# The x of three batches leaves attention as one float32 plane and is split where feed-forward first uses it

## The chip, the core and the metric

One core of a Trainium2 chip runs the whole program. The time is the device time of one execution in microseconds, and the kernel before is given by the median of three runs. An execution under the hardware profiler gives the busy times, waits and transfers that are read below.

## What is computed

Attention of 4 batches, 12 heads, 448 positions and 64 channels, in which the heads are mixed with each other before and after the softmax, is followed by a feed-forward layer whose activation is a rational function.

```python
def _attn_ref(q, k, v, w_pre, w_post) -> np.ndarray:
    scale = 1.0 / np.sqrt(q.shape[-1])
    scores = scale * np.matmul(q, k.transpose(0, 1, 3, 2))
    scores = np.einsum('bhij,hg->bgij', scores, w_pre)
    scores = scores - np.max(scores, axis=-1, keepdims=True)
    attn = np.exp(scores)
    attn = attn / (np.sum(attn, axis=-1, keepdims=True) + 1e-09)
    attn = np.einsum('bhij,hg->bgij', attn, w_post)
    return np.matmul(attn, v).astype(np.float32)

def _moe_ref(x, w_in, w_out, a, b) -> np.ndarray:
    h = x @ w_in
    h2 = h * h
    h3 = h2 * h
    P = a[0] + a[1] * h + a[2] * h2 + a[3] * h3
    Q = 1.0 + np.abs(b[0]) * np.abs(h) + np.abs(b[1]) * h2
    g = P / (Q + 1e-06)
    return (g @ w_out).astype(np.float32)
```

x is the output of attention with batches and positions joined: 1792 x 768. w_in is 768 x 2048, w_out 2048 x 768.

## The kernel before

**Order of the work.** The program is a list of operations, each with the engines that may do it, an estimated duration, what it depends on, and a time `at` by which it is due. `Plan.run` goes through them with simulated clocks: whenever an engine is free, it takes of the operations that are ready the one with the smallest `at`. Where several engines are allowed (`ON` names them), the first that is free takes it. What comes out is a fixed order of instructions for each engine; on the chip an engine runs its own order strictly, and an instruction whose operands are late holds up all behind it. `Ring` and `Slot` count the buffers of a pool in the same simulation.

**Attention.** The 1792 rows are cut into 16 tiles T, four to a batch b = T // 4, of 120 rows with one of 88 in each batch (T = 0, 7, 11, 15). For a tile, q times k gives scores in PSUM (L496); ScalarE or VectorE copies them to `st` (L236 and L238), and a DMA shuffles them into `d`, where heads and rows share the partitions. Then the tile goes through in groups of up to two blocks, 92 groups in all: TensorE mixes the heads into `ps_t` or `ps_u` (L565), VectorE takes the row maximum `nm` (L571), ScalarE the exponential `e` with its sum `sm` (L580), GpSimd adds 1e-9 to the sum (L587), VectorE takes the reciprocal `rr` (L591), GpSimd scales the second mixing matrix by it into `krs` (L600), TensorE mixes again with that (L640), and VectorE transposes the result into `aa` (L656). After the last group of a tile `put_av` multiplies by v (L705) into the pair of banks `ps_t` or `ps_u` that the mixing does not use at that time; when it has all three products, ScalarE copies each of two halves (`hv`) into the float32r buffer `xs` (L236, `hi`), VectorE subtracts that from PSUM into the plane beside it (L723, `lo`), and SP stores finished columns to `x_scr` in DRAM (L728).

**Products in pairs.** In feed-forward float32 accuracy comes from pairs: a value is its float32r copy ("hi") plus a remainder ("lo"), and a product is hi x hi + hi x lo + lo x hi. So x stands in two planes per half, `[128, hv, hi/lo, 3, 448]`, and so do the weights `w` and the activation `g`. The weights are prepared along the way from 64-bit inputs: ScalarE and VectorE bring them to `cm` (L405 to L430), ScalarE casts hi (L236), GpSimd subtracts lo (L446). These last make most of GpSimd's work in feed-forward.

**Feed-forward.** There are 64 units: four rounds over the four batches in the orders (0,3,1,2), (2,1,0,3), (3,0,1,2), (2,1,0,3), and four slices of the 2048 channels in each turn. A unit is 18 matmuls of 128x448 into `ps_s` (`m1`, L879), the rational function (ScalarE L892 to L919, VectorE L905 to L929, with `quot` at L929 last), the cast of its result to g's hi on ScalarE or VectorE (L236 or L238), the remainder of g on VectorE (L939), and 18 matmuls with w_out (`m2`, L969), due 2.5 units after the start of the unit's m1, so that the products of later units lie between. Batch 3 stays in `xs` and is the second turn. The others come from `x_scr` through `put_load_x(n)` (L860): n = 1 is batch 0 into the first score buffer, now named "x", due 45 us before the planned end of attention, n = 2 is batch 1 into "x", n = 3 is batch 2 into "xs"; n = 4 to 9 load a batch again in later rounds. A load takes both planes of a batch, 2.75 MB, at once:

```python
nc.sync.dma_start(out=t.bitcast(F32), in_=x_scr[b])
X[n] = t
```

PSUM has eight banks: `ps_s` and `ps_a` two each, `ps_t` and `ps_u` two each, which hold scores in attention and the sums over four units in feed-forward. Weight pieces come back from `w_scr` as `w` (L843), and a one-element memset on GpSimd (L833) holds each of the first of these loads back until an exponential late in attention is done.

Of the kernel before, what the change touches and what calls it, by code (L numbers as in the profile page):

```python
# [28 lines left out]
NT = 4 * B  # L29
# [178 lines left out]
def subs(n, on=("dve", "pool")):  # L208
# [5 lines left out]
    "s": ('act', 'dve'), "d_hi": ('act', 'dve'), "d_lo": ("dve", "pool"), "p": ("act", "dve"), "x_hi": ("act",),  # L214
    "g_hi": ("act", "dve"), "g_lo": ("dve",),
}


def dma(nbytes):
    return nbytes / 300e3  # L220
# [21 lines left out]
def mixed_attention_then_rational_ffn(ctx: ExitStack, tc, q, k, v, w, wmix, mask, a, b2, out):  # L242
# [447 lines left out]
    def put_av(T, pr, at):  # L690
# [19 lines left out]
        def part(hv):  # L710
            return box[hv][:, 0:3 * n].rearrange("p (r w) -> p r w", r=3)[:, :, 0:r]

        def hi(hv):
            def fn(eng):
                if hv == 0 and T % 4 == 0:
                    Xs[b] = sb["xs"].tile([128, 2, 2, 3, S], F32R, tag="xs", name="xs")
                move(nc, eng, Xs[b][:, hv, 0, :, c0:c0 + r], part(hv))
            return fn

        def lo(hv):  # L720
            def fn():
# [15 lines left out]
        for hv in range(2):  # L737
            deps, after = [o], []
            if hv == 0 and T % 4 == 0:
                deps.append(R["xs"].take())  # L740
            else:
                after.append(xs_op[b][0])
            h_ = add(copies(3 * n, False, on=ON["x_hi"]), 0, hi(hv), deps, at=at, after=after)
            l_ = add("dve", dve(3 * n), lo(hv), [h_], at=at)
            xs_op.setdefault(b, []).append(h_)
            x_done.setdefault((b, hv), []).append(l_)
            R["ps_" + holds[T]].uses[slots[hv].k].append(l_)
            if T % 4 > 1:
                last = T % 4 == 3
                cols, done = (slice(c0, S), x_done[b, hv][3:]) if last else (slice(0, c0 + r), x_done[b, hv][:])  # L750
                for hl in range(2):
                    when = at + (3.0 if last else 5.0) + (1.6 if last else 4.0) * (2 * hl + hv)
                    s_ = bulk(0.45, store(hv, hl, cols), done, at=when, nbytes=128 * 3 * max(cols.stop - cols.start, 240) * 4, late=1.0, since=when - 1.0)
                    x_st.setdefault(b, []).append(s_)
                    R["xs"].uses[b].append(s_)

    xs_op, x_done = {}, {}
    x_st = {}

# [91 lines left out]

    def put_load_x(n, at):
        b, name = homes[n]

        def fn():
# [4 lines left out]
            nc.sync.dma_start(out=t.bitcast(F32), in_=x_scr[b])  # L860
            X[n] = t
        x_ld[n] = [add(
            "sp", 0.63, fn, [R[name].take(), R["d"].uses[NT - 2] if n == 1 else op_rest, x_st[b]], at=at, extra=dma(128 * 2 * KD * S * 4))]
        x_use[n] = R[name].uses[-1]

    def put_unit(u):
# [254 lines left out]
```

## Time and profile before

| quantity | before |
|---|---|
| median of three runs | 831.5 us (831.42 to 833.6) |
| the profiled execution: its time | 830.89 us |
| its span | 829.1 us, granted clock 0.996 |
| TensorE (PE) busy | 801.0 us, 97% |
| weight loads (PEld) | 598.0 us, 72% |
| VectorE (DVE) | 690.6 us, 83% |
| ScalarE (ACT) | 502.4 us, 61% |
| GpSimd (POOL) | 222.2 us, 27% |
| DMA | 155.46 MB, mean 187 GB/s |

Attention fills the span up to about 350 us, feed-forward the rest. Busy time counts only instructions that compute, weight loads run beside matmuls, and a share is a mean over stages that have different limits. SP only issues transfers, which the DMA engines carry out.

### The profile page before, as it was taken

The numbers are of one execution on the slowest core, as the hardware profiler recorded it, in microseconds if no ns is written. First come the engines' busy times: TensorE is split into PE (matmuls) and PEld (weight loads), VectorE is DVE, ScalarE is ACT, GpSimd is POOL, SyncE is SP. The second block draws the span as 40 slices with busy tenths as digits, with TensorE's granted clock in tenths as the row PEclk, the third lists the DMA queues.
The fourth block names the chain that finished last, engine by engine and source line by source line (L and its number), as shares of the span: only waits on it lengthen the run. The fifth ranks groups of instructions, "written<-read, shape, count | busy, mean of one in ns | idle before, by whom it ended". The sixth has DMA issues, their size and how long they took to land.

```text
span 829.1 us, 23254 instructions
## 1 busy us (share of the span) xinstructions
PE 801.0 (97%) x9360; PEld 598.0 (72%) x9360; DVE 690.6 (83%) x1252; ACT 502.4 (61%) x1099; POOL 222.2 (27%) x393
## 2 busy tenths in 40 slices
PE   5889999999999999999999999999999999999998
PEld 1244455554554445589999999999999999999997
DVE  5677788887888888888999998999889999677775
ACT  2456666655665566566776775677557677545632
POOL 2224444432444343721111212123212222100000
PEclk9999999999999999999999999999999999999999
DMA  6677878777887675985733255664477634466314
GB/s 201 207 214 224 246 259 265 222 202 231 260 259 212 217 235 171 335 276 210 256 125 101 81 207 133 215 141 104 88 228 192 165 82 67 78 225 231 122 57 156
DMA packets 71900, 155.46 MB, mean 187 GB/s; under 512 B 12560, under 2 KB 52336, under 8 KB 70640
## 3 DMA queue, kind: packets, MB, share of 16 engines
q1 hardware_dynamic: 67736, 141.99, 52.6%
q0 software_dynamic: 3456, 11.01, 8.2%
q8 instruction: 74, 1.21, 0.6%
q10 hardware_dynamic: 600, 0.97, 0.4%
q14 instruction: 34, 0.28, 0.1%
HBM read 77.49 MB, written 37.75 MB: 139 GB/s over the span
## 4 chain that ended last, share of the span: by engine, by line
PE 84%; DMA 6%; DVE 5%; ACT 2%; issue 1%; POOL 0%; SPq 0%; ACTq 0%; DVEq 0%; POOLq 0%
PE ps_s L879 28%; PE ps_u L969 9%; PE ps_t L969 9%; PE ps_a L969 9%; PE ps_s L496 8%; PE ps_a L640 7%; PE ps_t L565 4%; PE ps_u L565 4%; DMA d<-st 4%; PE ps_u L705 2%; PE ps_t L705 2%; DVE nm L571 2%; ACT e L580 2%; DMA kk<-in_k 1%; DVE aa L656 1%
## 5 line engine op out<-in xcount | busy, mean ns | idle before, releaser
L656 DVE STREAM_TRANSPOSE aa<-ps_a 128x448 f32<-128x448 f32 (+1 forms) x184 | 107.8, 618 | 11.6 <-PE ps_a L640 10.8
L879 PE MATMUL ps_s<-d,w 128*128 128x448 f32 x504 | 107.4, 366 | 0.0
L879 PE MATMUL ps_s<-xs,w 128*128 128x448 f32 x504 | 107.1, 366 | 0.0
L236 ACT COPY st<-ps_s 120x448 f32<-120x448 f32 (+1 forms) x120 | 60.4, 533 | 69.2 <-PE ps_s L496 38.3
L496 PE MATMUL ps_s<-kk,q 64*64 64x448 f32 x720 | 94.0, 552 | 8.3 <-DMA kk<-in_k 5.4
L446 POOL TENSOR_TENSOR w<-cm,w 128x384 fp32r<-128x384 f32 x48 | 53.7, 1118 | 177.8 <-ACT w L236 168.4
L600 POOL TENSOR_SCALAR krs<-kpost,rr 128x64 f32<-128x64 f32 x180 | 81.7, 468 | 72.1 <-DVE rr L591 51.3
L879 PEld LDWEIGHTS ps_s<-d,w 128*128 128x128 f32 x504 | 94.3, 188 | 8.7 <-issue 0.9
L879 PEld LDWEIGHTS ps_s<-xs,w 128*128 128x128 f32 x504 | 94.6, 188 | 7.9
L640 PEld LDWEIGHTS ps_a<-e,krs 64*32 64x32 f32 x2880 | 44.7, 106 | 74.4 <-issue 29.0
L640 PE MATMUL ps_a<-e,krs 64*32 64x224 f32 x2880 | 92.6, 355 | 1.6 <-DVE aa L656 0.8
L892 ACT ACTIVATE m<-ps_s,a_sb 128x448 f32<-128x448 f32 x64 | 46.2, 722 | 76.8 <-PE ps_s L879 73.4
L969 PE MATMUL ps_u<-g,w 128*128 128x448 f32 x336 | 84.1, 366 | 0.0
L969 PE MATMUL ps_a<-g,w 128*128 128x448 f32 x336 | 84.1, 366 | 0.0
L969 PE MATMUL ps_t<-g,w 128*128 128x448 f32 x336 | 83.9, 365 | 0.0
L580 ACT ACTIVATE e<-ps_t,nm 128x448 f32<-128x448 f32 x92 | 57.8, 635 | 25.4 <-DVE nm L571 17.1
L580 ACT ACTIVATE e<-ps_u,nm 128x448 f32<-128x448 f32 x88 | 55.3, 635 | 22.0 <-DVE nm L571 18.6
L969 PEld LDWEIGHTS ps_t<-g,w 128*128 128x128 f32 x336 | 63.1, 188 | 5.3
L969 PEld LDWEIGHTS ps_a<-g,w 128*128 128x128 f32 x336 | 63.1, 188 | 5.2
L969 PEld LDWEIGHTS ps_u<-g,w 128*128 128x128 f32 x336 | 63.1, 188 | 5.2
L496 PEld LDWEIGHTS ps_s<-kk,q 64*64 64x64 f32 x720 | 29.5, 135 | 49.4 <-issue 21.5
L915 ACT ACTIVATE ua<-sq 128x448 f32<-128x448 f32 x64 | 37.1, 580 | 33.6 <-DVE sq L912 33.4
(90 smaller groups left out, 1452.7 us busy)
## 6 DMA issues: line engine op xcount, KB each, us to landing
d<-st SPq DMA_DIRECT2D x144, 210.0 KB
cr<-in_w SPq DMA_DIRECT2D x64, 384.0 KB
d<-x_scr SPq DMA_DIRECT2D x5, 2688.0 KB
xs<-x_scr SPq DMA_DIRECT2D x4, 2688.0 KB
o_scr<-o POOLq DMA_DIRECT2D x24, 448.0 KB, 5.7
d<-st SPq DMA_DIRECT2D x42, 157.5 KB
x_scr<-xs SPq DMA_DIRECT2D x12, 540.0 KB
q<-in_q SPq DMA_DIRECT2D x16, 384.0 KB
```

The lines of the kernel that those rows point to most:

```text
L236: eng.copy(o, i)
L446: eng.tensor_sub(t[:, 1, :], box["m"].bitcast(F32), t[:, 0, :].bitcast(F32))
L496: nc.tensor.matmul(box["s"][hh][i0:i1, 0:S], lhsT=Q[T][d, pr, i0:i1], rhs=K[b][d, pr, :], start=True, stop=True)
L565: nc.tensor.matmul(box[r if nt == 2 else 0]["t"][64 * c:64 * c + 64, 0:S], lhsT=kpre[p], rhs=Dt[T][p, kb + c if nt == 2 else kb, :], start ...
L580: nc.scalar.activation(e, box[r]["t"][:, 0:S], AF.Exp, bias=box[0]["nm"][:, r:r + 1], accum_out=box[0]["sm"][:, r:r + 1])
L600: eng.tensor_scalar_mul(box[r]["kr"], kpost, rr)
L640: nc.tensor.matmul(banks[c]["p"][q_:q_ + BT, JH * r:JH * (r + 1)], lhsT=box[r]["kr"][p, m_, :], rhs=box[r]["e"][p, JH * jh:JH * (jh + 1)], ...
L656: nc.vector.transpose(o, src)
L879: nc.tensor.matmul(h[:, 0:S], lhsT=W[fi][:, wi, kk * 128:(kk + 1) * 128], rhs=x[:, kk // 3, xj, kk % 3, :], start=(n == 0), stop=(n == 3 * ...
L892: nc.scalar.activation(new("m"), box["h"], AF.Identity, scale=a_sb[:, 3:4], bias=a_sb[:, 2:3])
L915: nc.scalar.activation(box["ua"], box["vv"], AF.Ln)
L969: nc.tensor.matmul(O[key][:, 0:S], lhsT=W[fi][:, wi, DM + m * 128:DM + (m + 1) * 128], rhs=box["g"][:, gi, :], start=(f == 0 and n == 0), ...
```

## The change

For batches 0, 1 and 2 (`whole`) the output of attention is copied from PSUM by ScalarE as before, but into one plain float32 plane `Y[b]`, one of two halves of the `xs` buffer by b % 2. The VectorE subtractions of these batches fall away (24 of 32). After the last tile of a batch six stores of 128x448 (224 KB each) bring the plane to `y_scr`, 18 in place of 24 stores of pieces to `x_scr`. Batch 3 is unchanged. At the first use of a batch in feed-forward (n = 1, 2, 3) SP loads the plane in two halves into the place of the remainders; ScalarE casts each of the six 128x448 pieces into the place of hi, and GpSimd subtracts that from the plane in place; two stores bring both planes to `x_scr` for the later rounds, which load them as before. The pieces are due 2.0 us apart from 20 us behind the load for n = 1, and 2.6 us apart from 6 us behind it for n = 2 and 3.

Counted over the program: ScalarE gets 18 casts and loses five score copies, which go to VectorE; VectorE also loses two casts of g and gains three copies of o; GpSimd gets 18 subtractions; SP issues six loads of y and six stores of x more, and three loads of x and six stores from attention fewer.

```diff
@@ put_av
+        whole = b < B - 1
+
         def hi(hv):
             def fn(eng):
                 if hv == 0 and T % 4 == 0:
-                    Xs[b] = sb["xs"].tile([128, 2, 2, 3, S], F32R, tag="xs", name="xs")
-                move(nc, eng, Xs[b][:, hv, 0, :, c0:c0 + r], part(hv))
+                    if b == 0 or not whole:
+                        Xs[b] = sb["xs"].tile([128, 2, 2, 3, S], F32R, tag="xs", name="xs")
+                    if whole:
+                        Y[b] = Xs[0].rearrange("p v l k s -> p (v l) k s").bitcast(F32)[:, 2 * (b % 2):2 * (b % 2) + 2]
+                move(nc, eng, Y[b][:, hv, :, c0:c0 + r] if whole else Xs[b][:, hv, 0, :, c0:c0 + r], part(hv))
             return fn
...
+        def store_y(hv, kk):
+            def fn():
+                nc.sync.dma_start(out=y_scr[b][:, hv, kk], in_=Y[b][:, hv, kk])
             return fn
...
-            l_ = add("dve", dve(3 * n), lo(hv), [h_], at=at)
+            l_ = h_ if whole else add("dve", dve(3 * n), lo(hv), [h_], at=at)
...
-            if T % 4 > 1:
+            if whole:
+                if T % 4 == 3:
+                    for kk in range(3):
+                        when = at + 3.0 + 1.6 * (3 * hv + kk)
+                        s_ = bulk(0.45, store_y(hv, kk), x_done[b, hv][:], at=when, nbytes=128 * S * 4, late=1.0, since=when - 1.0)
...
@@ put_load_x
-    def put_load_x(n, at):
+    def put_load_x(n, at, lead=0.0, gap=0.0):
...
+        if b in x_st:
+            x_ld[n] = [add("sp", 0.63, fn, [*free, x_st[b]], at=at, extra=dma(128 * 2 * KD * S * 4))]
+            return
...
+        def hi(hv, kk):
+            def fn(eng):
+                move(nc, eng, X[n][:, hv, 0, kk], X[n][:, hv, 1, kk].bitcast(F32))
...
+        def lo(hv, kk):
+            def fn(eng):
+                x = X[n][:, hv, 1, kk]
+                eng.tensor_sub(x, x.bitcast(F32), X[n][:, hv, 0, kk].bitcast(F32))
...
+        for hv in range(2):
+            got.append(bulk(0.5, load(hv), [*free, y_st[b]], at=at + hv, nbytes=128 * 3 * S * 4, after=got[:1]))
+            parts = []
+            for kk in range(3):
+                when = at + lead + gap * (3 * hv + kk)
+                h_ = add(copies(S, on=ON["x_hi"]), 0, hi(hv, kk), [got[hv]], at=when)
+                parts += [h_, add(subs(S, on=ON["x_lo"]), 0, lo(hv, kk), [h_], at=when)]
+            x_ld[n] += parts
+            s_ = bulk(0.63, store(hv), parts, at=at + lead + gap * (3 * hv + 3) + 2.0, nbytes=128 * 2 * 3 * S * 4)
...
@@ the calls
-        put_load_x(n, at=END1 + UNIT * PH * (held.index(n) - 1) + 1 if n > 1 else END1 - 45.0)
+        if n == 1:
+            put_load_x(n, at=END1 - 45.0, lead=20.0, gap=2.0)
+        else:
+            put_load_x(n, at=END1 + UNIT * PH * (held.index(n) - 1) + 1, lead=6.0, gap=2.6)
```

What this does to the orders is shown at three places; x2 and the like stand for equal instructions in a row, and the line numbers of the changed kernel are shifted by one or more.

VectorE at the end of tile 2, before (L723 is the two subtractions, L571 the row maxima, L238 a score copy):

```order
L591 RECIPROCAL rr<-sm 128x2
L723 TENSOR_TENSOR xs<-ps_u,xs 128x3x120 x2
L571 TENSOR_REDUCE nm<-ps_t 128x2
L656 STREAM_TRANSPOSE aa<-ps_a 128x2x7x32 x2
L571 TENSOR_REDUCE nm<-ps_u 128x2
L238 COPY st<-ps_s 120x448
L591 RECIPROCAL rr<-sm 128x2
L656 STREAM_TRANSPOSE aa<-ps_a 128x2x7x32 x2
```

The same place now:

```order
L592 RECIPROCAL rr<-sm 128x2
L572 TENSOR_REDUCE nm<-ps_t 128x2
L238 COPY st<-ps_s 120x448
L657 STREAM_TRANSPOSE aa<-ps_a 128x2x7x32 x2
L572 TENSOR_REDUCE nm<-ps_u 128x2
L592 RECIPROCAL rr<-sm 128x2
L657 STREAM_TRANSPOSE aa<-ps_a 128x2x7x32 x2
L572 TENSOR_REDUCE nm<-ps_t 128x2
L238 COPY st<-ps_s 120x448
```

The subtractions are gone, the reduction has moved up to their place, and a score copy has moved up behind it.

GpSimd at the end of attention, now (L908 is the subtraction of batch 0, L588 and L601 the norms of the last groups, L854 the memsets that pace the weight loads; before, only the norms and the memsets stand there):

```order
L601 TENSOR_SCALAR krs<-kpost,rr 128x64 x2
L908 TENSOR_TENSOR d<-d 128x448
L588 TENSOR_SCALAR sm<-sm 128x2
L854 MEMSET w_6186 1x1 x2
L908 TENSOR_TENSOR d<-d 128x448
L601 TENSOR_SCALAR krs<-kpost,rr 128x64
L588 TENSOR_SCALAR sm<-sm 128x2
L601 TENSOR_SCALAR krs<-kpost,rr 128x64
L854 MEMSET w_6186 1x1 x2
L908 TENSOR_TENSOR d<-d 128x448
```

Each subtraction now stands ahead of a norm. TensorE at the same place, before, with L879 the first feed-forward product:

```order
L705 MATMUL ps_u<-aa,vv 64x120 x28
L879 MATMUL ps_s<-d,w_6183 128x448 x18
L565 MATMUL ps_t<-d,kpre 64x448 x2
L640 MATMUL ps_a<-e,krs 32x224 x16
L705 MATMUL ps_u<-aa,vv 64x120 x28
L640 MATMUL ps_a<-e,krs 32x224 x16
```

And now:

```order
L706 MATMUL ps_u<-aa,vv 64x120 x28
L566 MATMUL ps_t<-d,kpre 64x448 x2
L641 MATMUL ps_a<-e,krs 32x224 x16
L706 MATMUL ps_u<-aa,vv 64x120 x28
L943 MATMUL ps_s<-d,w_6186 128x448 x18
L641 MATMUL ps_a<-e,krs 32x224 x16
```

The last mixing product, a second mixing and a product with v have moved ahead of the first feed-forward product, which waits for the whole split of batch 0.

ScalarE in feed-forward around units 4 and 5, now (L956 to L983 are the activations of a unit, `CAST d<-d` the casts of batch 1):

```order
L966 ACTIVATE sq<-sq,c_sb,b_sb 128x448
L236 CAST d<-d 128x448 x2
L956 ACTIVATE m<-ps_s,a_sb 128x448
L959 ACTIVATE sq<-ps_s 128x448
L962 ACTIVATE ua<-ps_s,b_sb 128x448
L411 ACTIVATE cm<-cr 128x384
L236 CAST w_6802<-cm 128x384
L979 ACTIVATE ua<-sq 128x448
L966 ACTIVATE sq<-sq,c_sb,b_sb 128x448
L983 ACTIVATE ua<-ua 128x448
L236 CAST d<-d 128x448
```

The casts stand between the activations of running units; before, there is nothing but those and the casts of weights and g.

## Rows read from the trace of the kernel before

**Rows 1.** Windows: from:to length, busy PE, PEld, DVE, ACT, POOL, clock, DMA share, GB/s.

```profile
60.00:310.00 250.00, 241.84 (x5304) 123.92 (x5304) 204.13 (x378) 155.94 (x418) 104.58 (x228) 1.00 0.77 235
375.00:705.00 330.00, 330.00 (x1624) 304.37 (x1623) 310.11 (x566) 225.01 (x426) 70.44 (x68) 1.00 0.53 150
```

**Rows 2.** Waits of TensorE, 60 to 310 us: waiter <- releaser: sum, count, mean.

```profile
PE ps_u L565 <- DVE nm L571: 1.5, 3, 0.7
PE ps_t L565 <- DMA d<-st: 1.4, 1, 1.4
PE ps_t L705 <- issue: 1.3, 1, 1.3
PE ps_u L565 <- DMA kk<-in_k: 1.0, 1, 1.0
PE ps_u L705 <- issue: 0.8, 1, 0.8
...
PE ps_u L565 <- DVE xs L723: 0.5, 1, 0.5
PE ps_t L565 <- DVE xs L723: 0.3, 1, 0.3
```

**Rows 3.** Timeline of VectorE, end of a tile: start, duration, instruction, [wait].

```profile
100.84 0.97 DVE L723 TENSOR_TENSOR xs<-ps_u,xs 128x360 fp32r<-128x360 f32 x2 [0.39 <-ACT xs L236]
101.73 1.08 DVE L571 TENSOR_REDUCE nm<-ps_t 128x2 f32<-128x896 f32 x1
```

**Rows 4.** Timeline of TensorE, right behind.

```profile
103.38 0.98 PE L565 MATMUL ps_u<-d,kpre 64*64 64x448 f32 x8 [0.73 <-DVE nm L571]
```

**Rows 5.** Lines, VectorE, 60 to 310 us: count | busy, mean ns | idle before.

```profile
L238 DVE COPY st<-ps_s 120x448 f32<-120x448 f32 (+1 forms) x45 | 27.5, 617 | 10.8 <-PE ps_s L496 6.8 <-DMA d<-st 3.0 <-PE ps_a L640 0.7
```

**Rows 6.** Lines by shape, ScalarE: the casts of g.

```profile
L236 ACT CAST g<-ua 128x448 fp32r<-128x448 f32 x32 | 18.2, 569 | 26.0 <-DVE ua L929 20.9 <-PE ps_a L969 4.8
```

**Rows 7.** Durations of the weight remainders on GpSimd: minimum/median/maximum ns.

```profile
L446 POOL TENSOR_TENSOR w<-cm,w x48: 997/1019/1650, 341.9 to 701.6; 128x384 fp32r<-128x384 f32 x48
```

**Rows 8.** Windows, end of attention.

```profile
335.00:350.00 15.00, 14.20 (x275) 8.24 (x275) 12.30 (x24) 8.77 (x23) 11.02 (x27) 1.00 1.01 363
```

**Rows 9.** Timeline of ScalarE, end of attention.

```profile
335.03 0.20 ACT L580 ACTIVATION_READ_ACCUMULATOR e<-ps_u,nm 128x1 f32 x1
```

**Rows 10.** Timeline of SP: the first two loads of x.

```profile
332.21 0.37 SPq L860 DMA_DIRECT2D d<-x_scr  x1
...
373.42 0.38 SPq L860 DMA_DIRECT2D d<-x_scr  x1
```

**Rows 11.** Windows, while that first load runs.

```profile
333.00:336.00 3.00, 2.38 (x44) 0.88 (x47) 2.93 (x6) 1.39 (x5) 2.47 (x3) 1.00 0.99 387
```

**Rows 12.** Timeline of TensorE: the first product with batch 1.

```profile
403.07 2.21 PE L879 MATMUL ps_s<-d,w 128*128 128x448 f32 x10
```

**Rows 13.** Windows, the units before that product.

```profile
380.00:412.00 32.00, 32.00 (x159) 29.44 (x158) 28.40 (x55) 24.66 (x49) 5.88 (x5) 1.00 0.61 214
```

**Rows 14.** Lines, VectorE, 375 to 705 us.

```profile
L929 DVE SCALAR_TENSOR_TENSOR ua<-m,a_sb,ua 128x448 f32<-128x448 f32 x46 | 39.3, 855 | 0.4
L912 DVE TENSOR_TENSOR sq<-sq,ua 128x448 f32<-128x448 f32 x46 | 31.4, 683 | 0.1
...
L238 DVE CAST g<-ua 128x448 fp32r<-128x448 f32 x20 | 13.3, 666 | 1.2
```

**Rows 15.** Lines, VectorE, 765 to 829 us, where GpSimd is silent.

```profile
L929 DVE SCALAR_TENSOR_TENSOR ua<-m,a_sb,ua 128x448 f32<-128x448 f32 x7 | 4.8, 683 | 0.1
...
L912 DVE TENSOR_TENSOR sq<-sq,ua 128x448 f32<-128x448 f32 x7 | 4.4, 622 | 0.1
...
L238 DVE CAST g<-ua 128x448 fp32r<-128x448 f32 x6 | 2.4, 394 | 1.1 <-PE ps_a L969 0.7
```

**Rows 16.** Lines, GpSimd, 375 to 705 us.

```profile
L446 POOL TENSOR_TENSOR w<-cm,w 128x384 fp32r<-128x384 f32 x43 | 48.6, 1130 | 167.7 <-ACT w L236 158.3 <-DVE ua L929 4.9 <-issue 4.5
```

**Rows 17.** Durations of the last step of the rational function on VectorE.

```profile
L929 DVE SCALAR_TENSOR_TENSOR ua<-m,a_sb,ua x64: 674/685/1474, 362.4 to 816.6; 128x448 f32<-128x448 f32 x64
```

More of the change, by code (lines that the diff above doesn't have):

```diff
@@ L214 @@
     "s": ('act', 'dve'), "d_hi": ('act', 'dve'), "d_lo": ("dve", "pool"), "p": ("act", "dve"), "x_hi": ("act",),
-    "g_hi": ("act", "dve"), "g_lo": ("dve",),
+    "g_hi": ("act", "dve"), "g_lo": ("dve",), "x_lo": ("pool",),
 }
@@ L293, in mixed_attention_then_rational_ffn @@
     x_scr = [dram.tile([128, 2, 2, 3, S], F32, name=f"x_scr{b}") for b in range(B)]
+    y_scr = [dram.tile([128, 2, 3, S], F32, name=f"y_scr{b}") for b in range(B - 1)]
     o_scr = [dram.tile([128, KD, S], F32, name=f"o_scr{b}") for b in range(B)]
@@ L739, in put_av @@
             if hv == 0 and T % 4 == 0:
-                deps.append(R["xs"].take())
+                if b == 0 or not whole:
+                    deps.append(R["xs"].take())
+                elif b > 1:
+                    deps.append(y_st[b - 2])
             else:
@@ L747, in put_av @@
             R["ps_" + holds[T]].uses[slots[hv].k].append(l_)
-            if T % 4 > 1:
+            if whole:
[3 more added lines that the diff above has]
+                        s_ = bulk(0.45, store_y(hv, kk), x_done[b, hv][:], at=when, nbytes=128 * S * 4, late=1.0, since=when - 1.0)
+                        y_st.setdefault(b, []).append(s_)
+                        R["xs"].uses[0].append(s_)
+            elif T % 4 > 1:
                 last = T % 4 == 3
@@ L754, in put_av @@
                     x_st.setdefault(b, []).append(s_)
-                    R["xs"].uses[b].append(s_)
+                    R["xs"].uses[-1].append(s_)
     xs_op, x_done = {}, {}
-    x_st = {}
+    x_st, y_st, Y = {}, {}, {}
     LEAD = {1: 15.0, 2: 9.0, 3: 15.0}
@@ L822, in mixed_attention_then_rational_ffn @@
     x_ld, m2_op, o_ev = {}, {}, {}
-    x_use = {0: R["xs"].uses[B - 1]}
+    x_use = {0: R["xs"].uses[-1]}
     x_ld[0] = x_done[B - 1, 0] + x_done[B - 1, 1]
@@ L859, in fn, with load, store @@
                 t = sb[name].tile([128, 2, 2, 3, S], F32R, tag=name, name=name)
-            nc.sync.dma_start(out=t.bitcast(F32), in_=x_scr[b])
             X[n] = t
-        x_ld[n] = [add(
-            "sp", 0.63, fn, [R[name].take(), R["d"].uses[NT - 2] if n == 1 else op_rest, x_st[b]], at=at, extra=dma(128 * 2 * KD * S * 4))]
+        def fn():
+            home()
+            nc.sync.dma_start(out=X[n].bitcast(F32), in_=x_scr[b])
+        free = [R[name].take(), R["d"].uses[NT - 2] if n == 1 else op_rest]
         x_use[n] = R[name].uses[-1]
+        if b in x_st:
+            x_ld[n] = [add("sp", 0.63, fn, [*free, x_st[b]], at=at, extra=dma(128 * 2 * KD * S * 4))]
+            return
+        def load(hv):
+            def fn():
+                if hv == 0:
+                    home()
+                nc.sync.dma_start(out=X[n][:, hv, 1].bitcast(F32), in_=y_scr[b][:, hv])
+            return fn
+        def hi(hv, kk):
+            def fn(eng):
+                move(nc, eng, X[n][:, hv, 0, kk], X[n][:, hv, 1, kk].bitcast(F32))
+            return fn
+        def lo(hv, kk):
+            def fn(eng):
+                x = X[n][:, hv, 1, kk]
+                eng.tensor_sub(x, x.bitcast(F32), X[n][:, hv, 0, kk].bitcast(F32))
+            return fn
+        def store(hv):
+            def fn():
+                nc.sync.dma_start(out=x_scr[b][:, hv], in_=X[n][:, hv].bitcast(F32))
+            return fn
+        x_ld[n], x_st[b] = [], []
+        got = []
+        for hv in range(2):
[7 more added lines that the diff above has]
+            s_ = bulk(0.63, store(hv), parts, at=at + lead + gap * (3 * hv + 3) + 2.0, nbytes=128 * 2 * 3 * S * 4)
+            x_st[b].append(s_)
+            x_use[n].append(s_)
     def put_unit(u):
```

3 lines of the change are left out of this document (2 added, 1 removed).

## Prediction, before the changed kernel was run

> **What bounds the kernel now.** I read the busy time by stretch first, because two stages with different limits share the span. From 375 to 705 us TensorE is busy for all 330.00 us while VectorE shows 310.11 of 330 [rows 1]: feed-forward is a chain of matmuls without a gap, and VectorE follows it with 6% to spare. From 60 to 310 us, in attention, TensorE is busy 241.84 of 250 us and VectorE 204.13 [rows 1]. So TensorE idles 8.2 us there, and only that idle time can be won in attention, whatever VectorE is spared.
>
> Next I asked what ended TensorE's waits between 60 and 310 us [rows 2]. The reduction for the row maximum (`nm`, L571) ended 1.5 us of them and the remainder of x itself (`xs`, L723) 0.5 and 0.3 us: 2.3 us that the change touches. Transfers of scores and keys ended 1.4 and 1.0 us, and 1.3 and 0.8 us are issue: 4.5 us that it does not touch. The other 1.4 us are small waits for ScalarE, for copies and for transposes. One tile end shows the mechanism: VectorE takes 0.97 us for the two remainders at 100.84 and only then the reduction, from 101.73 to 102.81 [rows 3]; TensorE starts the next mixing product at 103.38 after 0.73 us of idle time that `nm` ended [rows 4].
>
> **The change part by part.** *Attention.* Tiles 0 to 11 lose two VectorE subtractions each, 24 in all, by 0.97 us a pair [rows 3] about 12 us (six of them on the short tiles' smaller shape). ScalarE's copy out of PSUM stays, on the same shape, with a plain float32 output. The planner refills part of the room: five score copies go from ScalarE to VectorE, 5 x 0.617 = 3.1 us [rows 5]. VectorE is thus spared some 9 us, yet TensorE gains only where it waited. Low end: nothing, if these copies stand where the subtractions stood. High end: the whole 8.2 us. I take 3.5 us: the 2.3 us of direct waits and most of the 1.4 us that hang on the same VectorE queue. SP issues 18 stores in place of 24 for these batches, and they carry half the bytes; as no stall in rows 2 names an x store, I give that nothing, and what covers it is SP's idle time between shuffles.
>
> *The split itself.* Each of three batches now takes 6 ScalarE casts and 6 GpSimd subtractions on 128x448. The cast is priced by the nearest equal, 0.569 us [rows 6]. The subtraction does not stand in the trace at this size; at 128x384 it has minimum 0.997, median 1.019, maximum 1.650 us [rows 7], so by columns (x 448/384) 1.16 to 1.93, and I take 1.2, near the median.
>
> *Batch 0, in the tail of attention.* GpSimd is busy 11.02 of 15 us between 335 and 350 [rows 8]. Six subtractions are 7.2 us against 4.0 free: if all fall there, 3.2 us stick out; if the norms (`sm`, `krs`) they stand ahead of are early enough, nothing. ScalarE meets the first cast when it ends the exponentials at 335.2 [rows 9]. The load is issued at about 332.2, as today's [rows 10], behind a 384 KB weight load; at 387 GB/s [rows 11] the 384 and the first 672 KB end near 335.7, so ScalarE waits some 0.5 us, plus the cast, ahead of the next exponentials. I take +1.0 us for the tail, nearer to the low end because the planner also pulls the last mixing product and an AV ahead of the first feed-forward product, which gives the split time. TensorE has 0.8 us of idle time in this stretch [rows 8], too little to hide more.
>
> *Batches 1 and 2, in feed-forward.* Transfers first. The load for batch 1 can go at 373.42 [rows 10] and its first product starts at 403.07 [rows 12]: 29.6 us for a load half as long as now, six casts (3.4 us) and six subtractions (7.2 us). That is covered, and so is batch 2, a turn later. DMA is 0.61 busy from 380 to 412 us [rows 13]; the two changed loads save 2.75 MB and four stores add 5.5 MB, a net of some 7 us at rows 11's rate against 12.5 us free.
>
> What is not covered is VectorE. GpSimd's work lengthens it: with GpSimd on weight remainders (375 to 705 us) L929 takes 855, L912 683 and the cast of g 666 ns [rows 14]; where GpSimd is silent (765 to 829 us) 683, 622 and 394 [rows 15]. That is 46 x 0.172 + 46 x 0.061 + 20 x 0.272 = 16.2 us for 43 subtractions [rows 16], 0.38 us each, without the smaller lines. The longest L929 is 1474 against 674 ns [rows 17], so one can cost 0.8. I take 0.5 at 384 columns, 0.58 at 448: 12 x 0.58 = 7.0 us more VectorE time, most of it between 380 and 412, where VectorE has 32 - 28.4 = 3.6 us idle [rows 13]. ScalarE, busy 24.66 there [rows 13], gets 12 x 0.569 = 6.8 us and would fill 31.5 of 32. Low end 0, if each delay falls ahead of a g that is early; high end the full 7.0. Over the 3.6 us of cover stand 3.4, of which I take a little over half, **+1.9 us**, because the order of TensorE's products was made for these added operations and g's lead differs from unit to unit.
>
> The Trainium skill ("SBUF — State Buffer", "Who interferes with whom") says that a GpSimd instruction that reads SBUF and a VectorE instruction with two SBUF inputs, or in a two-port mode, hold one port pair exclusively, and the second waits for the whole first. By that rule the term would be 12 x 1.2 - 3.6 = 10.8 us; the trace agrees that the two lengthen each other, and differs in size.
>
> *Sum:* -3.5 + 1.0 + 1.9 = -0.6 us. The profiled execution took 830.89 us (span 829.1 and 1.8 around it), 0.6 under the median of the runs shown, 831.5; so 830.3 by the profile, and **830.9** beside the median. A measurement of this kernel can tell about 0.3%, 2.5 us, from no change.
>
> **Rivals.**
> *Attention's gain stays.* The 2.3 us of direct waits and 3.2 of the other 5.9 go, and tail and feed-forward hide their part: 831.5 - 5.5 = **826.0**. For it: the waits for `nm` follow the subtractions at once [rows 3, 4], and feed-forward absorbs some 16 us of lengthening today without a gap on TensorE [rows 1, 14, 15]. Against it: only 3.6 us of cover where twice that is added.
> *VectorE falls behind in feed-forward.* The six casts and six subtractions a turn come at three times the rate of today's GpSimd work; once VectorE's lag exceeds the lead of the tightest g, TensorE waits and, being full afterwards [rows 1], never regains it: -3.5 + 1.0 + 7.0 = +4.5, **836.0**. It decides from about 4 us of lag. For it: VectorE and ScalarE both stand near 32 of 32 us; against it: idle spots that follow TensorE's own pace move with it.
> *Each subtraction stops VectorE for its whole length:* 12 x 1.2 - 3.6 = 10.8, in all +8.3, **839.8**. Against it: 0.38 us by rows 14 to 16. This is the skill's rule above.
> *GpSimd in the tail is the wall:* +3.2 in place of 1.0: **833.1**.
> *Attention gains nothing,* since the score copies fill the gap: -3.5 falls away, **834.4**; that is the change not doing what it says.
>
> **How the numbers follow.** My forecast 0.35 (its own range 829.0 to 834.0), gain stays 0.33, VectorE behind 0.20, whole length 0.03, wall in the tail 0.03, no gain in attention 0.06. Faster by over 0.3%: 0.33 and 0.03 from the forecast's lower edge, 0.36. Slower by over 0.3%: 0.20 + 0.03 + 0.06 = 0.29. Within: 0.32 + 0.03 = 0.35. The range 825.0 to 837.5 leaves out the far side of the gain (up to 823.3) and the whole-length case, with some of "VectorE behind" (0.18 in all).
>
> **What would show it.** Right: TensorE's waits for `nm` and `xs` between 60 and 310 us shrink by about 2 us, the first feed-forward product starts some 2 us earlier, VectorE's two-input lines get longer between 380 and 412 us, and one or two gaps of 1 to 2 us stand on TensorE there, ended by `g`. Wrong: feed-forward without any gap (gain stays), gaps of 5 us and more (VectorE behind), TensorE waiting for `krs` between 335 and 350 us, or GpSimd subtractions well over 1.3 us.

## The result, and the profile after

| | before | changed |
|---|---|---|
| median of six runs | 831.46 us (828.74 to 833.6) | 838.95 us (835.47 to 841.51) |
| ratio | 1 | **1.0076**, 95% interval 1.0047 to 1.0106 |
| profiled execution: time, span | 830.89, 829.1 us | 835.47, 833.7 us |

The changed kernel is slower by 0.76%, by 3.9 to 8.8 us according to the interval. The prediction had 830.9 and a range up to 837.5; its rival "VectorE falls behind in feed-forward" had 836.0.

Head of the page of the changed kernel (busy us, share of the span, instructions):

```profile
PE 801.8 (96%) x9360; PEld 596.9 (72%) x9360; DVE 691.0 (83%) x1234; ACT 508.8 (61%) x1111; POOL 246.8 (30%) x411
```

The busy shares say almost nothing: VectorE is as busy as before although it has 24 subtractions fewer. The stretches say where it went. Windows of the changed kernel, columns as in [rows 1]:

```profile
60.00:310.00 250.00, 242.55 (x5328) 122.89 (x5328) 198.68 (x362) 153.67 (x414) 105.02 (x230) 0.99 0.72 222
375.00:705.00 330.00, 325.71 (x1597) 299.05 (x1596) 309.61 (x554) 227.34 (x430) 88.56 (x80) 1.00 0.55 159
335.00:350.00 15.00, 13.05 (x314) 7.91 (x298) 11.63 (x22) 8.79 (x23) 14.26 (x27) 0.89 0.85 297
380.00:412.00 32.00, 29.65 (x145) 26.70 (x144) 31.10 (x51) 22.32 (x43) 13.62 (x11) 1.00 0.66 232
```

From 60 to 310 us VectorE is spared 5.4 us (204.13 to 198.68), and TensorE's busy time grows by 0.7. These 0.7 us say little: cast16 and sub16_tail, kernels of the experiments below whose attention is ordered as here, show 241.87 and 237.65 us in the same window. In feed-forward TensorE, full before [rows 1], stands idle for 4.3 us, all of it where batches 1 and 2 are split: from 380 to 412 us VectorE has gone from 28.40 [rows 13] to 31.10 of 32 us with four instructions fewer. Three waits of TensorE from 375 us to the end (waiter, releaser: sum, count, longest) add up to that:

```profile
PE ps_t L1033 <- DVE g L1003: 2.2, 1, 2.2
PE ps_s L943 <- DVE m L972: 1.9, 1, 1.9
PE ps_t L1033 <- ACT g L236: 0.2, 1, 0.2
```

None of them is for a piece of x or for a weight, so TensorE does not wait for GpSimd's results themselves; it waits for what VectorE makes.

**Where the 4.6 us of span came from** can be read off three places of TensorE's timeline that both kernels pass. First, the mixing product that stands in both four groups before the end of attention (of before, then of the changed kernel):

```profile
332.88 0.98 PE L565 MATMUL ps_t<-d,kpre 64*64 64x448 f32 x8
```

```profile
330.44 0.98 PE L566 MATMUL ps_t<-d,kpre 64*64 64x448 f32 x8
```

Second, the last product with v; third, the last product of all. Before:

```profile
364.00 3.56 PE L705 MATMUL ps_u<-aa,vv 64*64 64x90 f32 x168
...
823.16 1.98 PE L969 MATMUL ps_a<-g,w 128*128 128x448 f32 x9
```

Changed:

```profile
363.25 3.56 PE L706 MATMUL ps_u<-aa,vv 64*64 64x90 f32 x168
...
827.86 1.98 PE L1033 MATMUL ps_a<-g,w 128*128 128x448 f32 x9
```

Attention up to its tail is 332.88 - 330.44 = 2.4 us shorter, the tail 1.7 longer (34.7 us from there to the end of the last product with v before, 36.4 now), and feed-forward, from 367.56 to 825.14 before and from 366.81 to 829.84 now, is 463.03 in place of 457.58 us: **5.4 us longer**. The sum is +4.7.

Of these three only feed-forward is more than executions differ by. With attention in the same order the mixing product starts at quite different times, in cast16 and then in sub16_tail:

```profile
330.39 0.98 PE L566 MATMUL ps_t<-d,kpre 64*64 64x448 f32 x8
```

```profile
337.44 0.98 PE L566 MATMUL ps_t<-d,kpre 64*64 64x448 f32 x8
```

So one execution of each kernel doesn't show what attention gained; the medians below have to. Of feed-forward's 5.4 us 4.3 are the three waits. The other 1.1 are busy time: the same 2251 products take 458.74 us in place of 457.58. What makes these stays open.

**What happens at the longest wait.** GpSimd, then VectorE of the changed kernel, around 396 us (start, duration, instruction):

```profile
394.42 1.02 POOL L447 TENSOR_TENSOR w<-cm,w 128x384 fp32r<-128x384 f32 x1 [1.04 <-ACT w L236]
395.40 3.00 POOL L908 TENSOR_TENSOR d<-d 128x448 fp32r<-128x448 f32 x2
```

```profile
394.79 1.13 DVE L993 SCALAR_TENSOR_TENSOR ua<-m,a_sb,ua 128x448 f32<-128x448 f32 x1
395.84 0.61 DVE L969 TENSOR_TENSOR m<-m,ps_s 128x448 f32<-128x448 f32 x1
396.38 1.03 DVE L976 TENSOR_TENSOR sq<-sq,ua 128x448 f32<-128x448 f32 x1
397.33 1.28 DVE L416 TENSOR_SCALAR cm<-cm 128x384 f32<-128x384 f32 x1
398.54 0.61 DVE L1003 TENSOR_TENSOR g<-ua,g 128x448 fp32r<-128x448 f32 x1
```

Two subtractions run from 395.40 to 398.40. Under them L969, which takes one operand from PSUM, keeps its 0.61 us; L976, with both from SBUF, takes 1.03, and the clamp of a weight, L416, 1.28 where its line had a mean of 0.354 before the change (380 to 436 us), and ends 0.2 us after the subtraction. Only then comes L1003, the remainder of g. It ends at 399.15, and TensorE goes on at 399.20:

```profile
396.57 0.47 PE L1033 MATMUL ps_t<-g,w 128*128 128x448 f32 x1 [0.19 <-ACT g L236]
399.20 1.29 PE L1033 MATMUL ps_t<-g,w 128*128 128x448 f32 x5 [2.16 <-DVE g L1003]
```

At the other long wait, which ends at 429.99 us, a subtraction from 426.15 to 427.52 stands beside L976 (1.05 us), and a weight's remainder that follows it at once on GpSimd (1.38 us) beside L1003 (1.41 us); `m` comes only behind these.

### The profile page after: what moved, and what is told of

Read it like the earlier page. It is cut to its first block, busy times and chain, and to the rows that moved or that the text cites. A ratio compares the mean times of both kernels' runs of the same rounds, so it can differ in the third digit from the quotient of the medians.

```text
span 833.7 us, 23258 instructions
## 1 busy us (share of the span) xinstructions
PE 801.8 (96%) x9360; PEld 596.9 (72%) x9360; DVE 691.0 (83%) x1234; ACT 508.8 (61%) x1111; POOL 246.8 (30%) x411
## 4 chain that ended last, share of the span: by engine, by line
PE 80%; DVE 9%; DMA 6%; ACT 3%; issue 2%; POOL 0%; SPq 0%; ACTq 0%; POOLq 0%; DVEq 0%
PE ps_s L943 25%; PE ps_u L1033 8%; PE ps_a L1033 8%; PE ps_t L1033 8%; PE ps_s L497 8%; PE ps_a L641 7%; PE ps_u L566 4%; PE ps_t L566 4%; PE ps_u L706 3%; DMA d<-st 2%; PE ps_t L706 2%; ACT e L581 2%; DVE nm L572 1%; DMA kk<-in_k 1%; DVE sq L976 1%
## 5 line engine op out<-in xcount | busy, mean ns | idle before, releaser
L236 ACT COPY st<-ps_s 120x448 f32<-120x448 f32 (+1 forms) x115 | 58.3, 533 | 75.4 <-PE ps_s L497 36.2
L601 POOL TENSOR_SCALAR krs<-kpost,rr 128x64 f32<-128x64 f32 x180 | 80.6, 461 | 69.9 <-DVE rr L592 52.3
L956 ACT ACTIVATE m<-ps_s,a_sb 128x448 f32<-128x448 f32 x64 | 46.3, 723 | 74.0 <-PE ps_s L943 73.3
L572 DVE TENSOR_REDUCE nm<-ps_t 128x2 f32<-128x896 f32 (+1 forms) x47 | 49.7, 1057 | 13.4 <-PE ps_t L566 11.9
```

What stands on the lines that cost most here:

```text
L236: eng.copy(o, i)
L572: nc.vector.tensor_reduce(out=nm[:, 0:nt], in_=box[0]["both"][:, 0:nt, 0:S], axis=AX.X, op=ALU.max, negate=True)
L601: eng.tensor_scalar_mul(box[r]["kr"], kpost, rr)
L956: nc.scalar.activation(new("m"), box["h"], AF.Identity, scale=a_sb[:, 3:4], bias=a_sb[:, 2:3])
```

## The experiments

The theory (A): GpSimd's subtractions lengthen VectorE, and VectorE has no cover for it where they stand. The first rival (B): it is ScalarE's casts, or the order made for them. Each kernel was timed against the kernel before on the same chip; that kernel had medians of 832.6 to 833.5 us there, so the ratios are compared, not the times. "Feed-forward" is the stretch measured above, in one profiled execution of each kernel; the two of the last version agree to 0.1 us.

| kernel | ratio to before, 95% interval | feed-forward, us |
|---|---|---|
| before | 1 | 457.6 |
| changed | 1.0076 (1.0047 to 1.0106) | 463.0 |
| sub16: all subtractions cut short | 0.9973 (0.9948 to 0.9998) | 457.6 |
| sub16_ff: those of batches 1, 2 cut short | 0.9987 (0.9964 to 1.0010) | 458.0 |
| sub16_tail: those of batch 0 cut short | 1.0064 (1.0034 to 1.0095) | 464.0 |
| cast16: casts of batches 0, 1 cut short | 1.0051 (1.0027 to 1.0074) | 464.5 |
| nosplit: no split at all | 0.9979 (0.9950 to 1.0009) | 459.0 |
| sub_dve: subtractions on VectorE | 1.0010 (0.9987 to 1.0032) | 459.6 |
| wlate_pool: weights eight units later | 1.0078 (1.0048 to 1.0109) | 465.0 |
| wlate_dve: that, subtractions on VectorE | 1.0053 (1.0025 to 1.0080) | 462.0 |
| b12_wlate_dve: that, batch 0 as before | 1.0082 (1.0052 to 1.0112) | 465.5 |
| w3_dve: weights three units later, VectorE | 1.0015 (0.9978 to 1.0052) | 458.2 |
| b12_w3_dve: that, batch 0 as before | 0.9969 (0.9937 to 1.0000) | 458.0 |
| b12_w3_again: the same once more | 0.9972 (0.9948 to 0.9997) | 458.0 |

### Is it the subtractions or the casts?

sub16, with every instruction in its place:

```diff
-                x = X[n][:, hv, 1, kk]
-                eng.tensor_sub(x, x.bitcast(F32), X[n][:, hv, 0, kk].bitcast(F32))
+                x = X[n][:, hv, 1, kk, 0:16]
+                eng.tensor_sub(x, x.bitcast(F32), X[n][:, hv, 0, kk, 0:16].bitcast(F32))
```

> Leaves out: the 18 GpSimd subtractions work on 16 of 448 columns, so the remainders of x are mostly wrong; the order on every engine and all transfers stay. Theory A (the subtractions lengthen VectorE in feed-forward and stand ahead of the norms in the tail): 829 to 832 us, no wait of TensorE for g or m between 380 and 436 us (4.2 us in the changed kernel), no wait for krs between 335 and 340 us (1.8 us). Theory B (the ScalarE casts and the order that was made for them cost the time): 836 to 839 us, and the waits for g and m stay.

cast16:

```diff
-                move(nc, eng, X[n][:, hv, 0, kk], X[n][:, hv, 1, kk].bitcast(F32))
+                s = slice(0, 16 if n < 3 else S)
+                move(nc, eng, X[n][:, hv, 0, kk, s], X[n][:, hv, 1, kk, s].bitcast(F32))
```

> Leaves out: the 12 ScalarE casts of batches 0 and 1 work on 16 of 448 columns (batch 2 keeps its six); the order on every engine and all transfers stay. Theory A: 837 to 839.5 us, the waits for g at about 397 us (2.2 us) and for m at about 430 us (1.9 us) both stay. Theory B: at most 835.5 us, the wait for g at about 397 us is gone and the one at 430 us, where batch 2 is still cast, stays.

sub16 has lost the whole slowdown: feed-forward is as long as before to 0.1 us, and TensorE waits for nothing in it. cast16 has kept it: its waits in feed-forward are the same two, one of them 0.6 us shorter:

```profile
PE ps_t L1034 <- DVE g L1004: 2.2, 1, 2.2
PE ps_s L944 <- DVE m L973: 1.3, 1, 1.3
```

Its ratio is 0.25% under that of the changed kernel, which the two intervals don't tell apart. That its feed-forward of 464.5 us is even longer than the changed kernel's comes of the clock behind the first wait (last section). Theory A holds, B falls. Since sub16 keeps the order, the two traces also give the price. Windows over feed-forward, of the changed kernel and of sub16:

```profile
366.81:829.84 463.03, 458.74 (x2251) 421.89 (x2250) 406.99 (x725) 293.76 (x547) 92.44 (x84) 1.00 0.52 154
```

```profile
371.45:829.01 457.56, 457.56 (x2251) 422.29 (x2250) 397.43 (x725) 292.75 (x547) 81.78 (x84) 1.00 0.52 156
```

The same 725 instructions of VectorE take 406.99 and 397.43 us: 9.6 us for 12 subtractions, **0.80 us each** in the mean, and a little more if the short ones lengthen anything. Lines of VectorE, changed kernel from 380 to 436 us, then sub16 from 384 to 440:

```profile
L976 DVE TENSOR_TENSOR sq<-sq,ua 128x448 f32<-128x448 f32 x7 | 6.6, 936 | 0.0
L431 DVE SCALAR_TENSOR_TENSOR cm<-cr,cg 128x384 int32<-128x384 int32 x8 | 6.3, 786 | 0.0
L993 DVE SCALAR_TENSOR_TENSOR ua<-m,a_sb,ua 128x448 f32<-128x448 f32 x7 | 6.3, 897 | 0.0
L1003 DVE TENSOR_TENSOR g<-ua,g 128x448 fp32r<-128x448 f32 x7 | 5.9, 848 | 0.0
L425 DVE SCALAR_TENSOR_TENSOR cg<-cr,cm 128x384 int32<-128x384 int32 x8 | 5.7, 716 | 0.0
...
L416 DVE TENSOR_SCALAR cm<-cm 128x384 f32<-128x384 f32 x8 | 4.4, 544 | 0.0
...
L972 DVE SCALAR_TENSOR_TENSOR m<-m,a_sb,ps_s 128x448 f32<-128x448 f32 x6 | 4.0, 671 | 0.0
```

```profile
L993 DVE SCALAR_TENSOR_TENSOR ua<-m,a_sb,ua 128x448 f32<-128x448 f32 x8 | 6.1, 756 | 0.1
L1003 DVE TENSOR_TENSOR g<-ua,g 128x448 fp32r<-128x448 f32 x9 | 5.5, 616 | 0.0
L972 DVE SCALAR_TENSOR_TENSOR m<-m,a_sb,ps_s 128x448 f32<-128x448 f32 x8 | 5.4, 673 | 0.0
L976 DVE TENSOR_TENSOR sq<-sq,ua 128x448 f32<-128x448 f32 x8 | 5.2, 652 | 0.0
L431 DVE SCALAR_TENSOR_TENSOR cm<-cr,cg 128x384 int32<-128x384 int32 x9 | 5.0, 552 | 0.0
...
L425 DVE SCALAR_TENSOR_TENSOR cg<-cr,cm 128x384 int32<-128x384 int32 x8 | 4.4, 550 | 0.0
L416 DVE TENSOR_SCALAR cm<-cm 128x384 f32<-128x384 f32 x9 | 3.6, 405 | 0.0
```

Over half of the price lies on lines that the prediction had set aside as smaller: L431, L425 and L416 of the weights and L1003, the remainder of g, together 8 x (0.234 + 0.166 + 0.139) + 7 x 0.232 = 5.9 us. L972, with an operand in PSUM, shows 671 and 673 ns: nothing.

### Feed-forward or the tail?

sub16_ff cuts short the subtractions of batches 1 and 2 alone (`s = slice(0, S if n == 1 else 16)`), sub16_tail those of batch 0 alone (`s = slice(0, 16 if n == 1 else S)`).

> Leaves out: the 12 GpSimd subtractions of batches 1 and 2 work on 16 of 448 columns; the six of batch 0 in the tail of attention are whole; the order on every engine stays. If batch 0's subtractions cost the tail some 3 us (1.8 of waiting for krs and 1.6 of a lower clock behind it): 834 to 836 us, 0.3 to 0.5% above the kernel with all 18 cut short (831.99), with the wait for krs and a granted clock near 0.9 from 335 to 350 us, and feed-forward as long as before the change. If the whole loss is made in feed-forward: 832 us.

> Leaves out: the six GpSimd subtractions of batch 0, in the tail of attention, work on 16 of 448 columns; the 12 of batches 1 and 2 are whole; the order on every engine stays. If the loss is made in feed-forward (5.4 us of 6.3): ratio to the kernel before 1.0045 to 1.007, feed-forward 462 to 465 us from attention's last product to the end, no wait for krs. If the tail makes half of it: 1.002 to 1.004.

sub16_tail keeps nearly all of the loss, sub16_ff has none of it in feed-forward. So the loss is made in feed-forward. What the tail adds is 0.14% by the first pair (0.9987 less 0.9973) and 0.12% by the second (1.0076 less 1.0064), about 1 us each, which neither pair can tell from nothing by its intervals. The mechanism of the tail is seen in the profile of the changed kernel, on GpSimd and then on TensorE:

```profile
336.18 1.52 POOL L908 TENSOR_TENSOR d<-d 128x448 fp32r<-128x448 f32 x1
337.68 0.75 POOL L601 TENSOR_SCALAR krs<-kpost,rr 128x64 f32<-128x64 f32 x1
```

```profile
338.49 1.46 PE L641 MATMUL ps_a<-e,krs 64*32 64x224 f32 x32 [1.82 <-POOL krs L601]
339.88 2.74 PE L706 MATMUL ps_u<-aa,vv 64*64 64x120 f32 x56
```

A subtraction stands ahead of the norm `krs`, and TensorE waits 1.82 us for it. sub16_ff has the same wait (1.8 us); sub16_tail has none for krs. From the mixing product to the last product with v three executions with batch 0's subtractions whole take 36.4, 36.9 and 37.0 us (changed, cast16, sub16_ff), two with them cut short 34.4 and 36.0 (sub16, sub16_tail, the latter with a wait of 1.8 us for which the profile shows no releaser).

### What does attention gain?

nosplit puts the plane into both places with two loads and does nothing more:

```diff
...
+            for l in range(2):
+                x_ld[n].append(bulk(0.5, plain(l), [*free, y_st[b]], at=at + l, nbytes=128 * KD * S * 4, after=x_ld[n][:1]))
+            return
```

> Leaves out: the split itself. Every load of batches 0 to 2 brings the plane twice, into both places, so no casts, no subtractions and no stores behind attention; feed-forward is ordered anew. It shows what attention alone gains. If the gain is the 3.5 us of the prediction: about 828 us. If all 8.2 us of idle time went: 823. If attention gains nothing, since score copies fill the room: 831.5. Theory A wants feed-forward without any wait of TensorE here.

Its ratio is 0.9979. sub16's is 0.9973 with a feed-forward as long as before, which puts attention's gain at about 2 us (0.2 to 4.3). nosplit's feed-forward is 1.5 us longer than before and has waits of 1.1 us for `m`, where theory A was said to want none: there is no split in it, so a new order alone can cost that much. Its gain ahead of feed-forward would then be some 3 us. By its interval nosplit alone doesn't exclude no gain. Waits of TensorE from 60 to 310 us, changed kernel, beside [rows 2]:

```profile
PE ps_u L566 <- DMA d<-st: 2.7, 1, 2.7
PE ps_t L706 <- issue: 1.6, 1, 1.6
PE ps_t L566 <- DMA q<-in_q: 0.7, 1, 0.7
PE ps_u L566 <- DMA y_scr<-xs: 0.7, 1, 0.7
```

No wait of TensorE for `nm` or for L723 is left. A new one stands in the last line: at 206.48 us, while SP issues the stores of batch 1, the profile puts a wait of a mixing product down to such a store: 0.7 us here, 0.8 to 1.2 in cast16, sub16_tail and nosplit, none in sub16 and sub16_ff. The product itself reads `d`, so how the store holds it up isn't shown. Other waits have grown: for score shuffles here, and for exponentials in other profiled executions with the same attention (2.2 us in sub16_tail, 3.4 in nosplit). Which comes differs between executions.

### Is it VectorE's missing cover, and can the change be had without the loss?

sub_dve gives the subtractions to VectorE (`"x_lo": ("dve",)`), the planner orders everything anew:

> The 18 subtractions go to VectorE, and everything is ordered anew; the output is the reference's. Theory A with its price (each GpSimd subtraction lengthens VectorE by about 0.63 us, as much as the subtraction costs there itself, some 0.61 us): feed-forward loses about as much as now, 4 to 6 us, the wait for krs in the tail is gone: 835 to 838 us. Rival (what hurts is that the order does not know of the lengthening, and an order that knows VectorE's load hides it): 829 to 833 us, at most one wait of TensorE under 1 us between 380 and 436 us.

At 1.0010, 832.3 us on a kernel before of 831.5, it came out on the rival's side: no wait of TensorE stands between 380 and 436 us. But it isn't without loss. VectorE does 12 subtractions of its own (0.61 us each), and feed-forward is 2.0 us longer than before, where it was 5.4 with GpSimd's. The order is another too, but the two ratios lie clear of each other, so helping VectorE with GpSimd was dearer here than not helping. wlate_pool leaves the subtractions on GpSimd and takes other work away from the place, the preparation of weights:

```diff
-            put_w(i // NCV, i % NCV, at=END1 + UNIT * u + 2.0, since=END1 + UNIT * u - 6.0)
+            due = END1 + UNIT * (u + 8.0 - u / 8.0)
+            put_w(i // NCV, i % NCV, at=due + 2.0, since=due - 6.0)
```

> The changed kernel with the preparation of weights in feed-forward started eight units later and ended two units later, so that VectorE and GpSimd do none of it while batch 1 is split and little while batch 2 is; the output is the reference's. If VectorE's missing cover makes the loss: feed-forward takes 458 to 460.5 us from the last product of attention to the end (463.0 in the changed kernel, 457.6 before), the tail loses as before, in all 833.5 to 836.5 us. If a single subtraction that stops VectorE at a late g is enough: waits of 2 us for g and m stay, 837 to 840 us.

Windows of the changed kernel and of wlate_pool, where batch 1 is split, and of wlate_pool later:

```profile
375.00:412.00 37.00, 34.65 (x169) 31.30 (x168) 36.10 (x60) 24.64 (x48) 14.39 (x12) 1.00 0.68 238
```

```profile
375.00:412.00 37.00, 37.00 (x183) 34.01 (x182) 31.36 (x48) 26.32 (x49) 12.22 (x10) 1.00 0.45 179
...
500.00:600.00 100.00, 97.79 (x480) 89.54 (x479) 89.13 (x165) 70.64 (x133) 24.15 (x24) 1.00 0.59 156
```

With 5.6 us of room on VectorE the subtractions of batch 1 cost TensorE nothing, in an order that is otherwise new. But there are new waits later on, for `m` above all (4.2 us in four), and the time is no better: feed-forward takes 465.0 us where 458 to 460.5 were expected, and the loss has moved. That the weights come bunched there is a guess that the windows don't bear out: from 500 to 600 us 15 weight pieces are prepared, 14 before the change, and VectorE is busy for 89.13 us, 92.69 before. What makes `m` late stays open. The two kernels with the same shift and the subtractions on VectorE also missed the totals expected of them: no idle time from 375 to 440 us, but 462.0 and 465.5 us of feed-forward. In b12_wlate_dve only batches 1 and 2 leave attention as plain planes:

```diff
-        whole = b < B - 1
+        whole = b in (1, 2)
...
-                    if b == 0 or not whole:
+                    if b != 2:
...
-                        Y[b] = Xs[0].rearrange("p v l k s -> p (v l) k s").bitcast(F32)[:, 2 * (b % 2):2 * (b % 2) + 2]
+                        Y[b] = Xs[1].rearrange("p v l k s -> p (v l) k s").bitcast(F32)[:, 2 * (b % 2):2 * (b % 2) + 2]
...
-                        R["xs"].uses[0].append(s_)
+                        R["xs"].uses[-1].append(s_)
```

> As the one with later weights, with the 18 subtractions on VectorE; the output is the reference's. Neither lengthening nor norms that wait for GpSimd: feed-forward within 1.5 us of the kernel before, the tail 1 to 2 us longer, attention 2 to 3 us shorter: 830.5 to 833 us. If the later weights make VectorE late elsewhere: waits for g after 480 us and 834 us or more.

> As the last, but only batches 1 and 2 leave attention as a plain plane; batch 0 is split in attention as in the kernel before, so the tail holds no split. The output is the reference's. Two thirds of attention's gain (1.5 to 2 us), a tail as before, feed-forward within 1.5 us of the kernel before: 829.5 to 832 us. If the tail's loss does not come from the split: no better than the last one.

The second was no better than the first, the sign that was to speak against the split as the tail's loss; with 3.5 us more of feed-forward than the first it can't tell.

A shift that is smaller and fades out was meant to keep the weights from bunching:

```diff
-            put_w(i // NCV, i % NCV, at=END1 + UNIT * u + 2.0, since=END1 + UNIT * u - 6.0)
+            due = END1 + UNIT * (u + max(0.0, 3.0 - u / 8.0))
+            put_w(i // NCV, i % NCV, at=due + 2.0, since=due - 6.0)
```

> All 18 subtractions on VectorE, and the first weights prepared up to three units later, fading out over 24 units, so that they do not bunch behind the split; the output is the reference's. If bunched weights made the loss of the kernel with eight units: feed-forward 457.5 to 460 us, ratio 0.997 to 1.001. If every shift of weights costs a wait for m: 1.003 or more.

> The same with batches 1 and 2 alone as plain planes, batch 0 split in attention as before. Tail as in the kernel before, two thirds of attention's gain of about 2 us, feed-forward 457.5 to 460 us: ratio 0.997 to 1.000. If feed-forward loses as much as attention gains: 1.000 to 1.003.

> The version with batches 1 and 2 as plain planes, subtractions on VectorE and weights up to three units later, once more against the kernel before, since its interval (0.9937 to 1.0000) ends at no change. If attention's gain of some 2 us is real and nothing is given back: ratio 0.996 to 0.999 again, feed-forward 457.5 to 458.5 us. If the first ratio was chance: 0.999 to 1.002.

All three have feed-forward without a wait of TensorE, 458.0 to 458.2 us. w3_dve has its feed-forward as expected, but its ratio, 1.0015, a little above what was expected. Its tail has 1.6 us of waiting for `sm` and 1.7 for exponentials between 330 and 375 us, which the kernel before hasn't (0.3 for exponentials). With batch 0 split in attention as in the kernel before the tail is as before (34.8 and 34.5 us, 34.7 before), and the version is faster than both kernels: **0.9972 (0.9948 to 0.9997)** in the repetition, 2.3 us under the kernel before by that ratio. Feed-forward and tail being as long as before, the gain should lie ahead of them, in attention. This is worked out and not seen: the two profiled executions reach the mixing product at 333.79 and 338.06 us, later than the 332.88 of the kernel before. Nor is the share of each step shown, since no run has batches 1 and 2 alone as plain planes without the later weights, or with the subtractions on GpSimd. The window where batches 1 and 2 are split, b12_w3_dve:

```profile
375.00:440.00 65.00, 65.00 (x320) 59.79 (x319) 62.06 (x120) 47.44 (x93) 10.93 (x8) 1.00 0.61 226
```

VectorE is busy for 62.06 of 65 us, and TensorE is full.

## Why the prediction was wrong

**What bounds the kernel** held: feed-forward is full on TensorE, VectorE follows it closely, and the time lost there was not regained.

**Attention, -3.5 us**: about -2 by sub16 (0.2 to 4.3 us of gain), some -3 by nosplit; the forecast's 3.5 lies inside both intervals, so that it was too high isn't shown. The 2.4 us of the two profiled executions are no evidence, since such executions differ by 7 us at that place. 1.2 of them stood already before the first x left attention (the product that starts at 58.35 us before starts at 57.16 now). The direct waits of 2.3 us went, as said. Of those that "hang on the same VectorE queue" nothing is seen, since transfers and exponentials end the waits there instead. The profile puts a wait of 0.7 us down to a store of the plane, a term that the prediction had at nothing.

**Tail, +1.0 us**: 1.7 in the profile, about 1 by the pairs. The size fits, the cause is another. The wait of ScalarE for the load didn't come: SP issued the loads at 325.49, not at 332.2, and the first cast started at 332.69 right behind the exponentials. What came is the subtraction ahead of `krs`, for which the text had 0 to 3.2 us and stayed near the low end. The first product of feed-forward started 2.7 us later than before (347.46 and 350.14 us), not some 2 us earlier: in the new order it stands behind more of attention.

**Feed-forward, +1.9 us, is the step that failed**: 5.4 in the profile. The mechanism was right: GpSimd's subtractions lengthen VectorE, and TensorE waits for `g` and `m`. Two sizes were wrong. One subtraction costs 0.80 us, not 0.58. The 0.38 from [rows 14 to 16] was the lengthening of three lines of VectorE, "without the smaller lines", and other lines carry over half of the price here. And of what stood over the cover "a little over half" was taken, on the thought that the order had been made for these operations; nearly all of it arrived. The planner's costs know nothing of the lengthening. With 0.80 and no halving the step's own sum gives 12 x 0.80 - 3.6 = 6.0, a forecast of 835.0, and the side would have been right.

That this sum comes near is partly luck. The 3.6 us are VectorE's idle time from 380 to 412 us, but only six of the twelve subtractions fell there; the others ran from 416 to 436 us, and ScalarE, for which 31.5 of 32 us were forecast, was busy for 22.32. Of the 9.6 us of lengthening 4.2 didn't reach TensorE, and from 375 to 440 us VectorE had 4.3 us idle before the change (60.69 of 65 busy). That it was this idle time that covered them isn't shown.

**The signs** that were named for the forecast came in kind: two gaps, of 2.2 and 1.9 us, in place of one or two of 1 to 2. The sign for VectorE falling behind, gaps of 5 us and more, didn't come. Each gap was small, but their sum is over twice the 1.9 us of the forecast.

**The rival that came nearest** in its parts is "VectorE falls behind in feed-forward", at 836.0; the total alone lies between this one and the 839.8 of the whole length. Its 7.0 us for feed-forward are 0.58 a subtraction without any cover, so a price that was too low and a cover left out made up for each other in part. Against it stood that feed-forward had absorbed some 16 us of lengthening so far; that says that there was cover, not that more was left.

**The rule of the Trainium skill** ("SBUF — State Buffer", "Who interferes with whom") that one of the two waits for the whole instruction of the other was given 0.03. The trace agrees with it on which instructions are hit: those with two inputs in SBUF and the short weight line L416 (544 against 405 ns), not L972 with one in PSUM; and the 1.28 us of L416 fit a wait to the end of the subtraction. The rival built on it charged every subtraction in full, 10.8 us in feed-forward, and was twice too high: subtractions of 1.3 us took 0.80 from VectorE in the mean. Some pass beside instructions that aren't hit, as the one beside L969 above, which kept its 0.61 us.

## What to carry to other kernels

An engine that is idle for most of the time is not free help if its instructions hold up the engine that it is to spare: price each by all lines that it lengthens, best with a kernel in which that instruction is cut short and nothing else moves. Where the engine that follows the bottleneck is over 90% busy, moved work needs room at its new place; here three units of delay for other work, with the subtractions on VectorE, brought feed-forward back to its old length, and eight units only moved the loss. Waits that are removed don't all come back as time, since other releases end new waits in the same stretch. And two profiled executions don't show a gain of 2 us in a stage where executions of one order differ by 7; only a stage that repeats to a fraction of a us can be read that way, the rest needs medians.

## What was not expected of the hardware

Behind the wait of 1.82 us in the tail the granted clock of TensorE was below full speed:

```profile
336.00:342.00 6.00, 4.18 (x90) 2.62 (x86) 4.93 (x9) 5.27 (x14) 5.77 (x13) 0.86 0.74 229
```

0.86 is a mean of the two levels, 1.2 and 2.4 GHz. The 56 products with v that follow took 2.74 us where they took 1.70 before, so the wait cost about 1 us more than its length there. In sub16_ff the same wait stood in a stretch with a granted clock of 1.00, and the 56 products took 1.72 us.

The wait for `g` of 2.16 us in feed-forward shows the same, the other way round. In the changed kernel the clock behind it was 1.00, in cast16, with a wait of the same length, 0.66 from 400 to 405 us. The next 18 products of the changed kernel and of cast16:

```profile
400.33 3.82 PE L943 MATMUL ps_s<-xs,d 128*128 128x448 f32 x18
```

```profile
400.75 5.37 PE L944 MATMUL ps_s<-xs,d 128*128 128x448 f32 x18
```

So a wait of some 2 us cost TensorE up to 1.6 us more than its length in some executions and nothing in others, and this is in the 464.5 us of cast16; sub16_tail, with 464.0, had a clock of 0.70 from 408 to 412 us. Why the clock fell in one execution and not in the other stays open.
